# C scaled in two stages, the last attention block in two query parts, and sums that begin in score steps: a planned kernel of state-space model and attention on one core

## The chip, the cores and the metric

The kernel runs on one core of a Trainium2 chip. The metric is the device time of one execution in microseconds (us), as the median of several runs. A core has five engines with a queue of instructions each: PE (TensorE, the matmuls), ACT (ScalarE), DVE (VectorE), POOL (GpSimd) and SP, which here issues most of the transfers.

## What is computed

Two parts that share nothing but the output array, side by side along its last axis.

```python
# A: a diagonal state-space model, L = 2048 steps, 640 states, 640 channels
Lam_bar = exp(dt * Lam);  B_bar = ((Lam_bar - 1) / Lam)[:, None] * Bmat
h = Lam_bar * h + x[t] @ B_bar.T            # complex, step by step
y = 2 * real(hseq @ Cmat.T) + x * Dskip
# B: attention, 32 heads of 20, one key and one value head for all of them
q = (x @ wq) per head;  k = x @ wk;  v = x @ wv
p = softmax(q k^T / sqrt(20));  out = (p v, heads joined) @ wo
```

## The kernel before

**A plan instead of loops.** `planned` (L547) runs a small simulation of the five engines on the host while the program is built. Processes hand in operations (`Op`) with a duration, dependencies and a priority; whenever an engine is free in the model, `pick` takes the ready one with the best priority; the order that comes out is the program, and `Emitter` puts the semaphores in. Durations, priorities and due times are numbers in the code: `STAGES` (L1444) sets some thirty of them anew at certain tile counts, `EARLIER` (L62) says by how many ns before its end an operation that reads PSUM frees its engine (8 for ACT), and a seed moves the due times of the background work by some tiles.

**Attention.** A *tile* is the scores of 128 keys by 512 queries for one head: 4 query blocks x 32 heads x 16 key chunks = 2048 tiles, in 32 blocks of 64 (four heads, 16 chunks). Two slots of three PSUM banks each (`SC0`, `SC1`) take turns. `fill` (L1482) writes two or three tiles of scores into a slot, in the rows of four 32-row matmuls (QT, KT) that run beside each other; ACT turns them into weights in PR by one exp of 1024 or 1536 columns (L1519). Some tiles go to DVE instead: a first pass (`fill_d`, L1717; the rows `BIG<-SC` and `BIG<-MB` of L864) adds and clamps the scores as integers, whose bits are then read as bf16, and three shifted copies follow, by DVE in pairs or singly (`BIG<-BIG`) or by POOL (L1834). Such a tile has four weighted sums with values scaled four ways (VS), a tile of ACT's one (VP). Where DVE's tile sits in the third bank of a slot, that slot's next fill waits for its first pass. `pv_source` (L1851) groups the weighted sums by four: 32-column matmuls beside each other that add up one block in the bank `pvbank` over all of its tiles. DVE copies the block out to `pvsb`, and denominators and head rows go over DRAM to the tiles OP (`normalize`); for the last two blocks `den_task` (L1976) does it on PE: a matmul with E gathers the denominators, DVE takes the reciprocal, a matmul with `ident` spreads it, and DVE multiplies by halves. `o_task` (L2009) multiplies by WO (by WOt, kept in BT, for the last two blocks); in the last query block the parts for output tiles 0, 2 and 4 that don't need the last block are summed early and parked in BA (`EARLY_O`).

**Background.** The state-space part runs as tasks of one PSUM bank each, taken by their due times, in tile numbers: units (x times B, rotation and scan on DVE) and the y sums. C is needed in two scaled forms, G2 C and G C (complex factors per state). `scale_c` (L2265) makes both on DVE, two scalings of four operations (`scaled`, L2226) for each of five chunks: CA gets G2 C, then CT is scaled in place by G, with scratch in W[1]. Only then, from tile 358 on, `cb_task` (L2308) multiplies CT with B: ten products CB, which y needs too. The load of WO is issued behind tile 200.

**Two modes of PE.** Score steps use 32-row tiles, nearly all else 32-column tiles; the plan charges for a change of mode. A task may put pieces of its sums into the free row of a score step (`ride`, `board`: a "ride"), but only after its first product has been made in a step of its own. `keep_source` (L936) adds empty matmuls (VZ) where PE has had little to do.

The lines that touch the prediction's steps most:

```python
            a = self.scaled(xa, x, sc[:, self.G2RE, c:c + 1], sc[:, self.G2IM, c:c + 1], True, (ck, ak), q, "qt", cts + [sc_op] + prev, 3)
            b = self.scaled(x, x, sc[:, self.GRE, c:c + 1], sc[:, self.GIM, c:c + 1], True, (ck, ck), q, "qt", a, 3)
...
            if r.last is None:
                continue
```

Of the kernel before, what the change touches and what calls it, by code (L numbers as in the profile page):

```python
# [46 lines left out]
class Schedule:  # L47
# [14 lines left out]
    EARLIER = {"dve": 40.0, "act": 8.0}  # L62
# [397 lines left out]
NTILE = NQB * NGG * NKC * 4  # L460
ALPHA = float(DH) ** -0.5
# [5 lines left out]
class Build:  # L467
# [45 lines left out]
    def lay_banks(self):  # L513
# [11 lines left out]
        self.rest, self.pvbank = rest, rest[-1]  # L525
        self.misc = rest[:self.MISC]
        self.early = [b for b in self.banks if b not in rest]

    def shared(self):
# [9 lines left out]
        shares.update({f"DR{self.NDS + i}": over for i, over in enumerate(self.dr_over)})  # L539
        shares["WOt"] = [f"BT{i}_{c}" for i in range(2) for c in range(NC)]  # L540
# [4 lines left out]
    SEEDS, REPLAYS = (10005,), 12  # L545
# [256 lines left out]
    def piece(self, r, out, lhsT, rhs, row):  # L802

        tag = object()
        r.end = tag
        at = slice(32 * row, 32 * row + 32)
        return lambda e: e.matmul(out, lhsT=lhsT[at], rhs=rhs[at], start=False, stop=r.end is tag,  # L807
                                  tile_position=(32 * row, 0), skip_group_check=True)

    def board(self, op, used):  # L810
# [5 lines left out]
        for r in self.rides:  # L816
            if r.last is None:
                continue
# [16 lines left out]
            fns = [self.piece(r, *m, x) for m in step[0]]  # L835
# [15 lines left out]
    OPEN = 1  # L851
# [15 lines left out]
    def program(self):  # L867
# [21 lines left out]
        self.pvq = {b: [[], [], [], []] for b in range(NQB * NGG)}  # L889
        self.pv_filled = {b: 0 for b in range(NQB * NGG)}  # L890
# [45 lines left out]
    def keep_source(self):  # L936

        b = self.pv_b
        if not self.started or b >= NQB * NGG or not all((b, j) in self.pv_first for j in range(4)):
            return None  # L940
        if self.pv_filled[b] == 64 and sum(len(q) for q in self.pvq[b]) < self.KEEP_Q:
            return None
# [80 lines left out]
    def loads(self):  # L1023
# [40 lines left out]
        for o, t in zip(self.vec_op + self.xn_op + [self.wk_op, self.wqa_op, self.wv_op, self.wq_op], self.LANDS):  # L1064
# [11 lines left out]
                       gate=lambda: self.tile_n > 200)  # L1076
# [358 lines left out]
    def rules(self):  # L1435

        while self.stages and self.stages[0][0] <= self.tile_n:
# [8 lines left out]
            648.138, 'WAITING': 3, 'REFILL': 905.623, 'SPARE': 148.045, 'LAG': 190.385, 'SOON': 2730.774, 'EARLIER': 4, 'LATER':  # L1446
            7, 'AHEAD': 10, 'CAP': 3, 'ROOM': 4, 'ALONE': 1.397, 'TASK': 0.95, 'PV': 2.034, 'EV': 0.52, 'P1': 0.5, 'COPY': 0.554,
            'COPY1': 0.836, 'P1OWN': 0.42, 'PVEV': 0.209, 'SCARCE': 8, 'BACKLOG': 9, 'GRACE': 55.439, 'SHARE': 0.29, 'MISC_FIRST':
            0}),
        (250, {'ALONE': 2.237, 'PV': 1.984, 'COPY1': 0.897}),  # L1450
        (500, {'STAY': 1.083, 'SPARE': 86.026, 'SOON': 2941.52, 'ALONE': 2.429, 'TASK': 0.989, 'PV': 1.9, 'P1': 0.519, 'PVEV':
            0.2, 'SCARCE': 7, 'BACKLOG': 7, 'SHARE': 0.301}),
        (850, {'STAY': 1.2, 'dve': 185.73, 'MARGIN': 628.898, 'REFILL': 766.143, 'SPARE': 148.045, 'LAG': 240.378, 'SOON':
            2730.774, 'ALONE': 1.449, 'TASK': 0.95, 'PV': 1.889, 'EV': 0.544, 'P1': 0.5, 'SCARCE': 8, 'BACKLOG': 9}),
        (1200, {'STAY': 0.876, 'MARGIN': 648.138, 'REFILL': 905.623, 'LAG': 190.385, 'ALONE': 2.13, 'PV': 1.718, 'EV': 0.506,
            'COPY': 0.534, 'COPY1': 0.9}),
        (1600, {'STAY': 1.2, 'pe': 196.33, 'EARLIER': 5, 'ALONE': 1.525, 'PV': 1.9, 'COPY': 0.554, 'COPY1': 0.897, 'P1OWN': 0.321,
            'GRACE': 41.523}),
# [23 lines left out]
    def fill(self, op, i):  # L1482
# [18 lines left out]
        for x, m in enumerate(tiles):  # L1501
            b, kc, j = self.score(op, m, t[:, 512 * x:512 * x + 512], banks[x])
            ents.append((b, kc, j, p.PR[:, h.index + x, :]))
# [26 lines left out]
        for (b, kc, j, rhs), key in zip(ents, keys):  # L1530
            self.pvq[b][j].append((p.VP[:, kc, 0:32], kc, rhs, key, ex, h, "VP"))
# [73 lines left out]
    def score(self, op, m, out, bank):  # L1605
# [5 lines left out]
        op.fns.append(self.mm(out, p.KT[32 * j:32 * j + 32, 128 * kc:128 * kc + 128],  # L1611
                              p.QT[32 * j:32 * j + 32, b % 12, :], True, True, tile_position=(32 * j, 0)))
        op.reads += [f"KT{kc // 4}", f"QT{b % 12}"] + ([f"QTr{b % 12}"] if b > 1 else [])
        op.writes.append(bank.key)
        return b, kc, j
# [101 lines left out]
    def fill_d(self, op, m, bank=None):  # L1717
# [8 lines left out]
        b, kc, j = self.score(op, m, bank.ap, bank)  # L1726
# [15 lines left out]
    def pv_entry(self, b, kc, j, k, h, op):  # L1742
        self.pvq[b][j].append((self.VS[:, k, kc, 0:32], kc, self.dr(h.index, BF16), f"DR{h.index}", op, h, "VS"))
# [19 lines left out]
    def copy_source(self):  # L1763
# [8 lines left out]
        if sum(len(d[2]) for d in can) < self.BACKLOG and not (can[0][3] == self.pv_b and self.pv_filled[self.pv_b] == 64):  # L1772
            return None
# [9 lines left out]
        if can[0][3] == self.pv_b and self.pv_filled[self.pv_b] == 64:  # L1783
# [8 lines left out]
    LAST = 16  # L1792
    POOL_LAST = 25
# [57 lines left out]
    def pv_source(self):  # L1851
        b = self.pv_b
        if b >= NQB * NGG or not self.started:
# [9 lines left out]
        for j in range(4):  # L1863
            can = [e for e in q[j] if e[4].end is not None and s.seen(e[4], "pe") <= t and self.vp_seen(e[1], t)]
# [4 lines left out]
        complete = self.pv_filled[b] == 64 and not any(self.d_left[b, j] for j in range(4))  # L1869
        left = sum(len(x) for x in q)  # L1870
        tight = self.tight()
        if len(group) < 4 and not tight and not (complete and left < 12 and len(group) == sum(1 for x in q if x)):
            return None
        prio = 0.9 if tight or complete else self.PV
# [6 lines left out]
    def pv(self, op, b, group):  # L1881
        p = self
        bank = self.pvbank
        for j, e in group:
# [4 lines left out]
            last = self.pv_filled[b] == 64 and not self.pvq[b][j] and not self.d_left[b, j]  # L1889
# [726 lines left out]
```

## Time and profile before

| what | us |
|---|---|
| median of three runs | 701.93 (701.88 to 702.15) |
| profiled execution: its time | 701.27 |
| its span, first to last instruction | 699.5 |
| first exp starts | 18.2 |
| last exp ends | 691.2 |

One execution was recorded. In the rows that the prediction shows, a group has its line, engine and operation, the tile written and those read, the shapes and a count, then the busy time in us and the mean duration of one in ns, and last the idle time of the engine just before them with what ended it. Rows in order of time begin with start and length in us, and an idle time in brackets. SC are the slots' banks, MB the two single ones. Matmuls that run beside each other in parts of the array have a row for each, so their durations don't add up to time.

### The profile page before, as it was taken

How to read it: one execution, taken by the hardware profiler on the slowest of the kernel's cores; microseconds unless marked ns; L12 is line 12 of the kernel's file. 1: busy time of each engine (PE TensorE's matmuls, PEld its weight loads, DVE VectorE, ACT ScalarE, POOL GpSimd, SP SyncE). 2: the span in 40 equal slices, each digit the busy share in tenths (PEclk: the TensorE clock that was granted, in tenths of full speed). 3: DMA queues.
4: the chain of work that ended last, by engine and by line, in shares of the span. 5: the costliest groups of instructions: out<-in, count | busy, mean ns of one | idle time of the engine just before them, and what ended most of it. 6: DMA issues, size and time to landing. Idle time of an engine off the chain costs nothing.

```text
span 699.5 us, 27013 instructions
## 1 busy us (share of the span) xinstructions
PE 684.9 (98%) x11350; PEld 248.1 (35%) x11350; DVE 630.2 (90%) x1211; ACT 685.4 (98%) x701; POOL 467.7 (67%) x796
## 2 busy tenths in 40 slices
PE   9999999999999999999999999999999999999997
PEld 5323232334323333534343323334333333343323
DVE  7899899999999988898979997899999999997695
ACT  7999999999999999999999999999999999999996
POOL 4266776443868898464777885767866777768780
PEclk9999999999999999999999999999999999999999
DMA  9649831101111111000030010120000011100101
GB/s 220 174 107 211 184 89 58 28 8 31 28 48 32 28 43 37 22 19 16 17 83 20 15 42 21 36 55 22 12 15 20 12 26 39 32 20 15 27 15 40
DMA packets 77590, 34.46 MB, mean 49 GB/s; under 512 B 58350, under 2 KB 77470, under 8 KB 77470
## 3 DMA queue, kind: packets, MB, share of 16 engines
q1 hardware_dynamic: 76506, 32.44, 19.3%
q8 instruction: 91, 1.49, 0.9%
q10 hardware_dynamic: 964, 0.29, 0.2%
q14 instruction: 29, 0.24, 0.1%
HBM read 11.53 MB, written 9.75 MB: 30 GB/s over the span
## 4 chain that ended last, share of the span: by engine, by line
PE 66%; ACT 33%; DVE 0%; issue 0%; DVEq 0%
ACT PR L1519 33%; PE MB L727 26%; PE MB L797 17%; PE SC L727 14%; PE MB L807 7%; PE SC L1155 1%; PE MB L723 1%; PE SC L723 0%; DVE PR L859 0%; PE MB L1272 0%; DVE mab L1161 0%; DVEq L510 0%; PE SC L1211 0%; DVE pvsb L859 0%; DVE M L863 0%
## 5 line engine op out<-in xcount | busy, mean ns | idle before, releaser
L1519 ACT ACTIVATE PR<-SC 128x1024 bf16<-128x1024 f32 (+1 forms) x677 | 670.5, 1177 | 4.0 <-PE SC L727 2.9
L1834 POOL INT64_ADD BIG<-BIG x761 | 455.4, 614 | 200.8 <-DVE BIG L864 71.8
L864 DVE TENSOR_SCALAR BIG<-SC 128x512 int16<-128x512 f32 x548 | 369.1, 684 | 48.9 <-PE SC L727 42.6
L727 PE MATMUL SC<-QT,KT 32*128 32x512 bf16 x2013 | 264.5, 384 | 7.0 <-ACT PR L1519 6.0
L727 PE MATMUL MB<-BIG,VS 128*32 128x512 bf16 x2332 | 257.4, 383 | 0.4 <-DVE pvsb L1901 0.2
L727 PE MATMUL MB<-PR,VP 128*32 128x512 bf16 x1465 | 213.7, 384 | 0.0
L727 PEld LDWEIGHTS SC<-QT,KT 32*128 32x128 bf16 x2013 | 66.6, 91 | 157.4 <-ACT PR L1519 94.5
L727 PEld LDWEIGHTS MB<-BIG,VS 128*32 128x32 bf16 x2332 | 61.6, 95 | 65.1 <-issue 40.2
L727 PEld LDWEIGHTS MB<-PR,VP 128*32 128x32 bf16 x1465 | 51.4, 94 | 44.6 <-issue 32.5
L797 PE MATMUL MB<-CT,W 128*32 128x320 bf16 (+2 forms) x996 | 52.6, 301 | 0.6 <-issue 0.6
L864 DVE TENSOR_SCALAR BIG<-BIG 128x1024 int16<-128x1024 int16 (+1 forms) x116 | 45.8, 427 | 1.7 <-PE MB L727 1.3
L807 PE MATMUL MB<-xaT,BT 32*128 32x256 bf16 x200 | 38.6, 272 | 0.7 <-ACT PR L1519 0.6
L797 PE MATMUL MB<-CA,W 128*32 128x512 bf16 (+1 forms) x640 | 35.5, 302 | 0.0
L797 PE MATMUL MB<-xaT,BA 128*32 128x256 bf16 x800 | 32.2, 275 | 0.0
L807 PE MATMUL MB<-diagD,xaT 32*128 32x128 bf16 x320 | 31.4, 217 | 0.0
L807 PEld LDWEIGHTS MB<-diagD,xaT 32*128 32x128 bf16 x320 | 17.7, 92 | 28.9 <-ACT PR L1519 19.3
L797 PEld LDWEIGHTS MB<-CT,W 128*32 128x32 bf16 x996 | 22.4, 96 | 15.2 <-issue 7.5
L2086 DVE CAST stg<-MB 128x512 bf16<-128x512 f32 x35 | 23.9, 682 | 2.5 <-PE MB L797 2.5
L797 PE MATMUL MB<-xaT,BT 128*32 128x256 bf16 x600 | 25.1, 274 | 0.0
L859 DVE TENSOR_TENSOR prod<-MB,tab 128x1024 bf16<-128x1024 f32 x20 | 24.3, 1217 | 0.4 <-PE MB L797 0.2
L864 DVE TENSOR_SCALAR BIG<-MB 128x512 int16<-128x512 f32 x35 | 23.8, 679 | 0.0
L2353 DVE TENSOR_TENSOR_SCAN g<-sc,hst,prod 128x256 bf16<-128x256 f32 x30 | 22.9, 774 | 0.1
(174 smaller groups left out, 488.3 us busy)
## 6 DMA issues: line engine op xcount, KB each, us to landing
out_dram<-stg SPq DMA_DIRECT2D x31, 128.0 KB, 1.8
qd<-BIG SPq DMA_DIRECT2D x20, 128.0 KB, 2.4
QT<-qd SPq DMA_DIRECT2D x28, 80.0 KB
OP<-pvsb SPq DMA_DIRECT2D x105, 20.0 KB
rdP<-recs SPq DMA_DIRECT2D x105, 20.0 KB
lbd<-BA SPq DMA_DIRECT2D x5, 320.0 KB, 4.0
CT<-in_B_x_dram SPq DMA_DIRECT2D x2, 640.0 KB, 5.3
BA<-in_A_B_re_dram SPq DMA_DIRECT2D x1, 800.0 KB, 7.0
```

The lines of the kernel that those rows point to most:

```text
L723: r = e.matmul(out[32 * j:32 * j + 32], lhsT=lhsT[:, 32 * j:32 * j + 32], rhs=rhs, start=start, stop=stop, tile_position=(0, 32 * j), skip ...
L727: return lambda e: e.matmul(out, lhsT=lhsT, rhs=rhs, start=start, stop=stop, **kw)
L797: x = e.matmul(out[32 * j:32 * j + 32], lhsT=lhsT[:, 32 * j:32 * j + 32], rhs=rhs, start=start, stop=r.end is tag, tile_position=(0, 32 * ...
L807: return lambda e: e.matmul(out, lhsT=lhsT[at], rhs=rhs[at], start=False, stop=r.end is tag, tile_position=(32 * row, 0), skip_group_check ...
L859: return lambda e: e.tensor_tensor(out, a, b, op)
L864: return lambda e: e.tensor_scalar(out, a, s1, s2, op0=op0, op1=op1)
L1155: prev = self.pe([lambda e, x=x, c=c, n=n, at=at: e.matmul(bank.cols(n * x, n * x + n), lhsT=p.wks[:, 128 * c:128 * c + 128], rhs=p.xbT[:, ...
L1519: ex = self.act(lambda e: e.activation(dst, t[:, 0:512 * n], ACT.Exp, scale=1.0 / UNIT), 0.8333 * 512 * n + 64, table="exp", deps=[op], re ...
L1834: op.fns.append(lambda e: e.int64_add(words(dst), words(src), add))
L2086: ev = self.dve(lambda e: e.tensor_copy(st, bank.ap), 645, deps=[prev], reads=[bank.key], writes=[key], prio=self.EV, gate=(lambda: last.e ...
L2353: o = self.dve(lambda e, ri=ri, init=init: e.tensor_tensor_scan(p.g[:, u, ri, :], rdec, p.prod[:, 1, 0, ri, :], init, ALU.mult, ALU.add), ...
```

## The change

1. **C in two stages.** CA gets G C first, for all five chunks; CB is made from CA. The second stage scales CT in place by G2, at a lower priority, due at tile 400, with scratch in WO, so WO is loaded only after it. CB is due from tile 172 on. The y sums take the two forms from the other array each.
2. **The tail in two query parts.** The last block's tiles are 256 queries of two key chunks, so that one half of the queries is complete after half of the block's tiles; evacuation, denominators and output of the halves are apart. Only output tiles 2 and 4 have an early part; tiles 0 and 1 wait for the left half alone.
3. **Sums may begin in score steps** (`BEGIN`): the first piece of a task may be a ride.
4. **The model takes an exp at full length** (`EARLIER` of ACT 0 instead of 8 ns), other numbers in `STAGES`, and another seed.

```diff
-    EARLIER = {"dve": 40.0, "act": 8.0}
+    EARLIER = {"dve": 40.0, "act": 0.0}
...
-    SEEDS, REPLAYS = (10005,), 12
+    SEEDS, REPLAYS = (169732,), 12
...
-            if r.last is None:
+            if r.last is None and (not self.BEGIN or any(d.end is None or s.seen(d, "pe") > s.t for d in r.bank.last)):
                 continue
...
-            fns = [self.piece(r, *m, x) for m in step[0]]
+            fns = [self.piece(r, *m, x, start=r.last is None and not i) for i, m in enumerate(step[0])]
...
-                       gate=lambda: self.tile_n > 200)
+                       gate=lambda: self.c_more is not None and self.s.done(self.c_more))
...
-        (1200, {'STAY': 0.876, 'MARGIN': 648.138, 'REFILL': 905.623, 'LAG': 190.385, 'ALONE': 2.13, 'PV': 1.718, 'EV': 0.506,
-            'COPY': 0.534, 'COPY1': 0.9}),
+        (1200, {'STAY': 0.876, 'PAUSE': 500.0, 'dve': 233.993, 'MARGIN': 696.79, 'REFILL': 905.623, 'LAG': 230.879, 'SOON':
+            2154.193, 'ALONE': 2.13, 'PV': 1.756, 'EV': 0.506, 'COPY1': 0.9, 'PVEV': 0.2, 'BACKLOG': 8}),
...
+    @staticmethod
+    def parts(b, r):
+
+        if b < LASTB:
+            return [(0, r, 0, 512)]
+        return [(256 * x, 2 * (r % 8) + x, 256 * (r // 8), 256) for x in range(2)]
...
-    LAST = 16
-    POOL_LAST = 25
+    LAST = 12
+    POOL_LAST = 14
...
+            elif b == LASTB:
+                ev = self.dve(lambda e: e.tensor_copy(p.pvsb[:, 1, 0:256], bank.cols(0, 256)), 380, deps=[op], reads=[bank.key],
+                              writes=["pvsb1"], prio=self.PVEV, gate=free)
             else:
-                self.evac_op[b] = [
-                    self.act(lambda e: e.activation(p.pvsb[:, slot, :], bank.ap, ACT.Copy), 600, deps=[op],
-                             reads=[bank.key], writes=[f"pvsb{slot}", f"pvsb{slot}r"], prio=0.1, gate=free)]
+                ev = self.act(lambda e: e.activation(p.pvsb[:, 1, 256:512], bank.cols(256, 512), ACT.Copy), 380, deps=[op],
+                              reads=[self.pvright], writes=["pvsb1r"], prio=0.1)
...
-    EARLY_O = (0, 2, 4)
+    EARLY_O = (2, 4)
...
-            a = self.scaled(xa, x, sc[:, self.G2RE, c:c + 1], sc[:, self.G2IM, c:c + 1], True, (ck, ak), q, "qt", cts + [sc_op] + prev, 3)
-            b = self.scaled(x, x, sc[:, self.GRE, c:c + 1], sc[:, self.GIM, c:c + 1], True, (ck, ck), q, "qt", a, 3)
-            prev = b
-            ops += a + b
+            prev = self.scaled(xa, x, sc[:, self.GRE, c:c + 1], sc[:, self.GIM, c:c + 1], True, (ck, ak), q, "qt",
+                               list(self.ct_op) + [sc_op] + prev, 3)
+            ops += prev
+        more = []
+        for c in range(NC):
+            x, ck = p.CT[:, :, c, :], [f"CT0_{c}", f"CT1_{c}"]
+            prev = self.scaled(x, x, sc[:, self.G2RE, c:c + 1], sc[:, self.G2IM, c:c + 1], True, (ck, ck), p.WO[:, 0:2, :], "qc",
+                               [sc_op] + prev, 3.4)
+            more += prev
+        self.c_more = more
+        self.s.spawn(self.hurry(self.C2_DUE, more))
...
-    CB_FROM, CB_STEP = 358.689, 15.665
+    C_DUE, C2_DUE = 200, 400
+    CB_FROM, CB_STEP = 172.381, 11.308
...
-                    m, mk = (p.CT, f"CT{ri}_{c}") if eo else (p.CA, f"CA{c}")
+                    m, mk = (p.CA, f"CA{c}") if eo else (p.CT, f"CT{ri}_{c}")
```

Three places show how the order moves. **DVE, before, in the last third of the scaling.** A row has line, operation, tile written and tiles read, and its size; `CA<-CT,sc` and `CT<-CT,sc` are products with the factors, W is scratch.

```order
L864 TENSOR_SCALAR W<-CT,sc 128x1280
L859 TENSOR_TENSOR OP<-OP,rdP 128x512
L864 TENSOR_SCALAR BIG<-BIG 128x2x512
L863 TENSOR_SCALAR CA<-CT,sc 128x2x640
L859 TENSOR_TENSOR prod<-prod 128x512
L859 TENSOR_TENSOR CA<-CA,W 128x640
L859 TENSOR_TENSOR CA<-W,CA 128x640
L2353 SCALAR_TENSOR_TENSOR g<-sc,prod 128x256
L864 TENSOR_SCALAR W<-CT,sc 128x1280
L863 TENSOR_SCALAR CT<-CT,sc 128x2x640
```

**DVE, after, the end of the first stage**, the fifth chunk:

```order
L867 TENSOR_SCALAR W<-CT,sc 128x1280
L867 TENSOR_SCALAR BIG<-SC 128x512
L866 TENSOR_SCALAR CA<-CT,sc 128x2x640
L867 TENSOR_SCALAR BIG<-SC 128x512 x2
L1316 CAST BIG<-MB 128x512
L862 TENSOR_TENSOR CA<-CA,W 128x640
L867 TENSOR_SCALAR BIG<-SC 128x512
L862 TENSOR_TENSOR CA<-W,CA 128x640
```

Two scalings stood close together without a first pass (`BIG<-SC`) between them; now four first passes stand inside one scaling, and the scalings of the second stage (`WO<-CT,sc`) follow between later ones. In all, 47 first passes stood between the first and the last scaling operation of 40; now 32 stand inside the first stage and 34 inside the second.

**ACT, before, exps 104 to 146**, and then **after, exps 104 to 149**; 128x1024 is a two-tile exp, 128x1536 a three-tile one:

```order
L1519 ACTIVATE PR<-SC 128x1024 x6
L1519 ACTIVATE PR<-SC 128x1536
L1519 ACTIVATE PR<-SC 128x1024 x5
L1519 ACTIVATE PR<-SC 128x1536 x2
L1519 ACTIVATE PR<-SC 128x1024 x2
L1519 ACTIVATE PR<-SC 128x1536 x10
L1519 ACTIVATE PR<-SC 128x1024 x5
L1519 ACTIVATE PR<-SC 128x1536 x8
L1519 ACTIVATE PR<-SC 128x1024 x4
```

```order
L1527 ACTIVATE PR<-SC 128x1536
L1527 ACTIVATE PR<-SC 128x1024 x7
L1527 ACTIVATE PR<-SC 128x1536
L1527 ACTIVATE PR<-SC 128x1024 x2
L1527 ACTIVATE PR<-SC 128x1536
L1527 ACTIVATE PR<-SC 128x1024 x3
L1527 ACTIVATE PR<-SC 128x1536 x3
L1527 ACTIVATE PR<-SC 128x1024 x14
L1527 ACTIVATE PR<-SC 128x1536 x5
L1527 ACTIVATE PR<-SC 128x1024 x9
```

Of 43 exps 21 had three tiles; of 46 now 11 have.

**PE, before, behind the last weighted sum** (`PR,VP`), and then **after**; `E` gathers denominators, `ident` spreads their reciprocals, `WO,OP` and `BT,pvsb` are the output's sums:

```order
L727 MATMUL MB<-PR,VP 32x512 x3
L723 MATMUL SC<-WO,OP 32x512 x16
L723 MATMUL SC<-BT,pvsb 32x512 x4
L723 MATMUL SC<-E,pvsb 32x4 x16
L723 MATMUL SC<-WO,OP 32x512 x12
L727 MATMUL SC<-ident,rdT 32x128 x16
L723 MATMUL SC<-WO,OP 32x512 x4
L723 MATMUL SC<-BT,pvsb 32x512 x12
L723 MATMUL SC<-BT,pvsb 32x128 x16
L723 MATMUL SC<-BT,pvsb 32x512 x8
```

```order
L1943 MATMUL MB<-PR,VP 32x256 x4
L726 MATMUL SC<-WO,OP 32x512 x16
L726 MATMUL SC<-E,pvsb 32x4 x8
L726 MATMUL SC<-BT,pvsb 32x512 x8
L726 MATMUL SC<-WO,OP 32x512 x4
L726 MATMUL SC<-ident,rdT 32x128 x8
L726 MATMUL SC<-WO,OP 32x512 x12
L726 MATMUL SC<-BT,pvsb 32x128 x16
L726 MATMUL MB<-BT,pvsb 32x512 x4
L726 MATMUL SC<-BT,pvsb 32x512 x8
L726 MATMUL SC<-WO,OP 32x512 x16
L726 MATMUL SC<-BT,pvsb 32x512 x8
```

The denominators' matmuls are half as many, the output sums of tiles 0, 1 and 3 stand whole behind the last weighted sum, and those of tile 3 come last.

More of the change, by code (lines that the diff above doesn't have):

```diff
@@ L460 @@
 NTILE = NQB * NGG * NKC * 4
+LASTB = NQB * NGG - 1
 ALPHA = float(DH) ** -0.5
@@ L1910, in pv, with pv_fn, fn @@
             self.pv_gate = list(self.evac_op[b])
+    def pv_fn(self, b, j, v, kc, rhs, first, last):
+        p, bank = self, self.pvbank
+        parts = self.parts(min(b, LASTB), kc)
+        def fn(e):
+            for i, (lo, c, at, n) in enumerate(parts):
+                r = e.matmul(bank.tensor[32 * j:32 * j + 32, bank.off + at:bank.off + at + n], lhsT=v[:, c, 0:32], rhs=rhs[:, lo:lo + n],
+                             start=first and not i, stop=last and i == len(parts) - 1, tile_position=(0, 32 * j), skip_group_check=True)
+            return r
+        return fn
     LATE_DMA = 2000.0
```

167 lines of the change are left out of this document (95 added, 72 removed).

## The prediction

> **What bounds the kernel now.** First the page's busy shares and its groups, then ScalarE's exps apart by shape, then the stretch from the first exp to the last beside the end behind it.
>
> ```profile
> PE 684.9 (98%) x11350; PEld 248.1 (35%) x11350; DVE 630.2 (90%) x1211; ACT 685.4 (98%) x701; POOL 467.7 (67%) x796
> ...
> L1519 ACT ACTIVATE PR<-SC 128x1024 bf16<-128x1024 f32 (+1 forms) x677 | 670.5, 1177 | 4.0 <-PE SC L727 2.9
> ```
>
> ```profile
> L1519 ACT ACTIVATE PR<-SC 128x1024 bf16<-128x1024 f32 x566 | 532.9, 1106 | 4.0 <-PE SC L727 2.9 <-PE MB L727 0.7
> L1519 ACT ACTIVATE PR<-SC 128x1536 bf16<-128x1536 f32 x111 | 160.2, 1538 | 0.0
> ```
>
> ```profile
> 18.00:691.50 673.50, 664.39 (x11113) 236.34 (x11113) 614.01 (x1151) 670.48 (x677) 459.62 (x769) 1.00 0.19 44
> 691.50:699.50 8.00, 3.94 (x108) 1.81 (x100) 2.89 (x6) 1.79 (x3) 0.00 (x0) 0.92 0.29 84
> ```
>
> The columns of the last fence are length, then busy us of PE, PEld, DVE, ACT, POOL, then granted clock, DMA share, GB/s. Two engines show 98%, but matmul ends are modelled, so PE's figure proves little. ACT's does: 677 exps in one row, with 4.0 us of idle time in all. What one exp occupies isn't its mean duration, since neighbours overlap; it comes from a run of equal ones:
>
> ```profile
> 18.16 22.11 ACT L1519 ACTIVATE PR<-SC 128x1024 bf16<-128x1024 f32 x24 [1.45 <-PE SC L727]
> ```
>
> These 24, all of two tiles, take 22.11 us: **0.92 us for a two-tile exp**. A three-tile one lasts 1538 - 1106 = 0.43 us longer, so **1.35**. Check: 566 x 0.92 + 111 x 1.35 = 520.7 + 149.9 = 670.6, the busy time of the row. The exp row therefore *is* the stretch, and the stretch is 96% of the span.
>
> Does PE have room beside it? One cycle near the end:
>
> ```profile
> 667.30 0.39 PE L727 MATMUL SC<-QT,KT 32*128 32x512 bf16 x3
> 667.62 0.39 PE L727 MATMUL MB<-PR,VP 128*32 128x512 bf16 x1
> ...
> 667.85 0.38 PE L727 MATMUL MB<-BIG,VS 128*32 128x512 bf16 x1
> ...
> 668.17 0.39 PE L727 MATMUL SC<-QT,KT 32*128 32x512 bf16 x3
> ```
>
> Scores start at 667.30, two groups of four sums follow at 667.62 and 667.85, and the next scores start at 668.17: 0.87 us with some 0.1 us of waiting, against 0.92 for the exp. A third group adds about 0.22 and overshoots. So ACT leads, and PE is close behind.
>
> Last, the hole where ACT does what DVE can't:
>
> ```profile
> L864 DVE TENSOR_SCALAR W<-CT,sc x10: 527/539/903, 86.7 to 156.6; 128x1280 bf16<-128x1280 bf16 x10
> ```
>
> ```profile
> L1519 ACT ACTIVATE PR<-SC 128x1536 bf16<-128x1536 f32 x21 | 28.9, 1571 | 0.0
> L1519 ACT ACTIVATE PR<-SC 128x1024 bf16<-128x1024 f32 x14 | 13.7, 1158 | 0.0
> ```
>
> ```profile
> 123.00:163.00 40.00, 37.10 (x645) 14.80 (x645) 38.51 (x82) 39.99 (x35) 15.93 (x26) 1.00 0.11 26
> ```
>
> C is scaled from 86.7 us until about 159. From 123 to 163 DVE is busy 38.51 of 40 us, and 21 of 35 exps have three tiles: DVE has no time for its third of the tiles, so ACT pays 1.35 us for three tiles where 0.92 would do.
>
> **The change, part by part.**
>
> *Exps.* Counted in the order, 566 + 111 become 579 two-tile, 98 three-tile and 1 one-tile exp; 1465 tiles become 1453. At 0.92, 1.35 and 0.92 - 0.43 = 0.49 us: 532.7 + 132.3 + 0.5 = 665.5, against 670.6. **-5.1 us**, on the path, and certain as far as ACT stays without gaps. The rows quoted with the change show where: 11 three-tile exps stand where 21 did. The model's own numbers (the ACT entry of `EARLIER`, the stages' table, the seed) issue nothing: what they do is in these counts. The work of scaling is as large as before; only half of it stands ahead of the CB products, and the other half lies between DVE's first passes.
>
> *DVE.* Its part of the tiles grows by 12:
>
> ```profile
> L864 DVE TENSOR_SCALAR BIG<-SC 128x512 int16<-128x512 f32 x548 | 369.1, 684 | 48.9 <-PE SC L727 42.6 <-PE MB L727 0.6
> ...
> L864 DVE TENSOR_SCALAR BIG<-BIG 128x1024 int16<-128x1024 int16 x111 | 44.8, 434 | 1.7 <-PE MB L727 1.3
> ...
> L864 DVE TENSOR_SCALAR BIG<-BIG 128x512 int16<-128x512 int16 x5 | 1.2, 278 | 0.0
> ```
>
> 12 first passes x 0.67 (369.1/548) = 8.1; 16 more pair copies x 0.40 = 6.5; 4 more single copies x 0.24 = 1.0; less about 0.7 at the end: +15 us, since POOL's copies stay at 761. DVE's 614 become 629 in a stretch of some 668: its idle time falls from 59 to 39 us. Hidden as long as no bank waits for a first pass.
>
> *PE.* In matmuls of 512 columns: scores stay 2048; weighted sums rise by 36 (three more for each of 12 tiles); of the other column-tiled work, 40 move into free rows of score steps (275 to 315, since sums may begin there), where they cost nothing. Net -4, or -1 group. Fillers, which only keep PE active, fall by 88 of 256 columns:
>
> ```profile
> L727 PE MATMUL MB<-KT,VZ 128*32 128x256 bf16 x228 | 10.1, 274 | 0.0
> ```
>
> 22 groups at about 0.11: -2.4 us, of which nothing counts where PE waited anyway. So PE's useful work stays while ACT's falls by 5.1: **PE's lead over the exps shrinks**. I let ACT's idle time rise from 4.0 to 4.5 (+0.5). The bounds: -2, if rides and the early CB products fill the gaps better; +5, the whole gain of ACT, if PE keeps its pace.
>
> *The end.* Behind the last exp stand:
>
> ```profile
> 688.39 2.85 ACT L1519 ACTIVATE PR<-SC 128x1536 bf16<-128x1536 f32 x2
> ...
> 695.99 0.60 ACT L2081 ACTIVATE PR<-SC 128x512 bf16<-128x512 f32 x1 [0.46 <-PE SC L723]
> ```
>
> ```profile
> 690.59 0.60 PE L727 MATMUL MB<-BIG,VS 128*32 128x512 bf16 x8
> ...
> 691.51 1.04 PE L723 MATMUL SC<-WO,OP 128*32 128x512 bf16 x16
> ...
> 693.78 1.75 PE L723 MATMUL SC<-BT,pvsb 128*32 128x512 bf16 x36
> ```
>
> 16 matmuls take 1.04 and 8 take 0.60, so four take 0.22. The end now is 8.3 us (691.24 to 699.5), and PE runs 691.51 to 695.53, 4.0 us, of which 15 groups (60 matmuls, with 16 of 128 columns as four) are 3.3: the rest waits for the normalizing chain. After the change 20 groups stand there (48 of WO, 32 of BT): output tile 0 has no early part any more. 4.4 us plus some 0.25 for the denominators: 4.65, with no waiting, since the left half's work fills the right half's chain. **+0.6**. Bounds: -0.8, if the shorter chain (256 columns in evacuation and product, a one-tile last exp) is what counts, and +1.2, if both add up.
>
> *Moved transfers.* The WO load leaves its place on SP's queue:
>
> ```profile
> L797 PE MATMUL MB<-WO,OP x436: 219/379/391, 227.4 to 584.5; 128*32 128x512 bf16 x77, 128*32 128x128 bf16 x69
> ...
> L707 SPq DMA_DIRECT2D WO<-in_B_wo_dram x1: 425/425/425, 97.4 to 97.4; - x1
> ```
>
> Now it follows the second stage, which ends behind 121 of 595 first passes, a fifth of the way, near 155 us (18 + 673 x 0.2). First use is at 227.4, at almost the same score number (627 against 621). Some 70 us cover it: nothing. The sums of y now wait for the second stage too, but the first of them stand behind 690 of 2048 scores, a third of the way, so nothing queues there either.
>
> *Sum.* -5.1 + 0.5 + 0.6 = -4.0. Profiled execution: 701.27 - 4.0 = 697.3. The median of the runs, 701.93, is 0.66 above that execution, so I forecast **697.9**.
>
> **Rivals.**
>
> *PE takes over as the bound.* For it: the 0.87 us cycle, useful work that stays. Against it: 4.0 us of idle ACT time at almost the same PE load. Then only the fillers' 2.4 and the one group come off, with the end's +0.6: 701.93 - 2.6 + 0.6 = **699.9**.
>
> *DVE takes over, slower.* Where a fill's third bank holds DVE's tile, the bank comes free by DVE's first pass; a late pass holds the fill and so ACT. For it, in the last stages ACT loses most:
>
> ```profile
> 508.00:578.00 70.00, 69.56 (x1113) 23.94 (x1101) 68.56 (x126) 69.64 (x73) 49.66 (x84) 1.00 0.07 19
> 578.00:648.00 70.00, 68.98 (x1185) 24.64 (x1185) 63.97 (x117) 68.56 (x71) 52.31 (x89) 1.00 0.11 28
> ```
>
> Against it: at 68.56 us of DVE in 70 ACT lost 0.36 us, and the 1.44 fall where DVE had six to spare. If every 70 us lost 1.44, 9.6 such stretches lose 13.8 instead of 4.5: 697.9 + 9.3 = **707.2**. It is slower than before from an ACT idle time of about 10 us on.
>
> *TensorE loses its clock.* Fillers fall by 22 groups. In the table the clock is 1.00 through the stretch and 0.92 only behind the last exp, where PE works 3.94 of 8 us. At half clock the streaming part of a cycle, 3 x 0.21, doubles: 0.87 becomes 1.5, and 7 us of exps take 4.5 more: 697.9 + 4.5 = **702.4** for one such stretch, and two are clearly slower. Against it, the stretch that lost fillers, 123 to 163 us, now has CB products instead. The Trainium skill speaks for this rival: its page "TensorE: Matmul & The Clock Gate", section "What's actually happening", says that the gate falls to half after an idle window of about 3.4 us. The trace shows no such drop ahead of 691.5, so what counts as idle inside a dense stretch no run here shows.
>
> *The end gains instead*, with -0.8 there and 2 us less idle: 701.93 - 5.1 - 2 - 0.8 = **694.0**.
>
> **How the numbers follow.** Forecast 60%, its own range 695.5 to 700; PE bound 17% (699 to 701.5); DVE late 12% (703.3 to 707); clock 4%; the better end 7%. The range leaves out the upper part of DVE's case, most of two clock drops and a sliver at the low end: 694.3 to 702.5. A measurement here can tell 0.2%, 1.4 us, so "same" is 700.5 to 703.3. Faster: 60 + 7 + 10 of PE's 17 = 77%. Same: the other 7 and, of the clock's 4, 3: 10%. Slower: 12 + 1 = 13%.
>
> **What would show it.** Right: exps of 579, 98 and 1 in a busy row near 665.5 with 3 to 6 us of idle time; few three-tile exps between 123 and 163 us; the last exp ending near 686.6; 8 to 9.5 us behind it with PE busy throughout; PE's clock 1.00. Wrong: idle ahead of the exps over 10 us, released by PE behind long runs of sums (PE's rival) or with PE's scores waiting for DVE's first passes (DVE's); a stretch under clock 1.00; an end under 8 us. The forecast falls if ACT's idle time takes back the 5.1.

## The result and the profile after

The changed kernel takes **697.84 us** (median of 5 runs, 696.98 to 698.27), the kernel before 701.93 (701.61 to 702.21, 5 runs): a ratio of 0.9943, 95% interval 0.9932 to 0.9954. The profiled execution took 697.64 us, its span is 695.8; the one of before took 701.27, with a span of 699.5, so the two profiles are 3.7 apart where the medians are 4.1 apart.

The page after, busy time of the engines and the group of all exps (last the idle time ahead of them, with what ended it):

```profile
PE 684.4 (98%) x11492; PEld 251.8 (36%) x11492; DVE 637.2 (92%) x1243; ACT 681.9 (98%) x703; POOL 469.0 (67%) x796
...
L1527 ACT ACTIVATE PR<-SC 128x1024 bf16<-128x1024 f32 (+1 forms) x678 | 666.6, 1130 | 4.1 <-PE SC L1623 2.9
```

The same group after, by shape:

```profile
L1527 ACT ACTIVATE PR<-SC 128x1024 bf16<-128x1024 f32 x579 | 544.6, 1067 | 3.6 <-PE SC L1623 2.5 <-PE MB L1623 0.3 <-PE MB L1943 0.2
L1527 ACT ACTIVATE PR<-SC 128x1536 bf16<-128x1536 f32 x98 | 141.5, 1506 | 0.5 <-PE SC L1623 0.4
L1527 ACT ACTIVATE PR<-SC 128x512 bf16<-128x512 f32 x1 | 0.7, 698 | 0.0
```

The counts are the forecast's. The busy time is 666.6 where it said 665.5, the idle time 4.1 where it said 4.5. Now the stretch of the exps, the end behind it, and the former hole (columns as before: length, busy us of PE, PEld, DVE, ACT, POOL, granted clock, DMA share, GB/s):

```profile
18.60:687.90 669.30, 662.41 (x11248) 238.84 (x11244) 621.86 (x1185) 666.60 (x678) 460.91 (x769) 1.00 0.19 44
687.90:695.80 7.90, 4.98 (x118) 2.74 (x110) 1.92 (x4) 2.17 (x4) 0.00 (x0) 1.00 0.30 85
...
123.00:163.00 40.00, 39.61 (x640) 14.12 (x636) 36.08 (x73) 40.00 (x40) 22.65 (x39) 1.00 0.19 46
```

The stretch from the first exp's start (18.69) to the last one's end (687.90) is 669.2 us, it was 673.1: **-3.9**. The end is 7.9, it was 8.3: **-0.4**. The first exp starts 0.5 later, with the same order of instructions on ACT, DVE and POOL ahead of it; in the profiles of all runs here it starts between 18.0 and 18.9, so that is scatter. From 123 to 163 us DVE is busy 36.1 us instead of 38.5, PE 39.6 instead of 37.1, and 10 of the 40 exps have three tiles, where 21 of 35 had.

### The profile page after: what moved, and what is told of

Read it like the earlier page. It is cut to its first block, busy times and chain, and to the rows that moved or that the text cites. A ratio compares the mean times of both kernels' runs of the same rounds, so it can differ in the third digit from the quotient of the medians.

```text
span 695.8 us, 27396 instructions
## 1 busy us (share of the span) xinstructions
PE 684.4 (98%) x11492; PEld 251.8 (36%) x11492; DVE 637.2 (92%) x1243; ACT 681.9 (98%) x703; POOL 469.0 (67%) x796
## 4 chain that ended last, share of the span: by engine, by line
PE 57%; ACT 41%; DVE 1%; issue 0%
ACT PR L1527 41%; PE MB L1943 21%; PE MB L800 14%; PE SC L1623 10%; PE MB L810 8%; PE MB L730 1%; DVE BIG L867 1%; PE SC L1159 1%; PE SC L726 1%; PE MB L726 0%; PE SC L730 0%; DVE pvsb L1922 0%; PE MB L1276 0%; DVE mab L1165 0%; DVE prod L862 0%
## 5 line engine op out<-in xcount | busy, mean ns | idle before, releaser
L1527 ACT ACTIVATE PR<-SC 128x1024 bf16<-128x1024 f32 (+1 forms) x678 | 666.6, 1130 | 4.1 <-PE SC L1623 2.9
L867 DVE TENSOR_SCALAR BIG<-SC 128x512 int16<-128x512 f32 x560 | 376.1, 684 | 37.7 <-PE SC L1623 32.0
L1943 PE MATMUL MB<-BIG,VS 128*32 128x512 bf16 (+1 forms) x2468 | 269.5, 376 | 0.9 <-DVE pvsb L1922 0.9
L1623 PE MATMUL SC<-QT,KT 32*128 32x512 bf16 (+1 forms) x2073 | 265.6, 378 | 4.4 <-ACT PR L1527 1.8
L1943 PE MATMUL MB<-PR,VP 128*32 128x512 bf16 (+1 forms) x1495 | 222.2, 378 | 0.1
L1943 PEld LDWEIGHTS MB<-BIG,VS 128*32 128x32 bf16 x2468 | 68.3, 95 | 65.1 <-issue 40.4
L867 DVE TENSOR_SCALAR BIG<-BIG 128x1024 int16<-128x1024 int16 (+1 forms) x136 | 52.3, 418 | 0.9 <-PE MB L1943 0.4
L800 PE MATMUL MB<-CA,W 128*32 128x320 bf16 (+2 forms) x992 | 51.5, 300 | 0.8 <-DVE BIG L2363 0.4
L810 PE MATMUL MB<-xaT,BT 32*128 32x256 bf16 x192 | 37.1, 273 | 0.0
L800 PE MATMUL MB<-CT,W 128*32 128x512 bf16 (+1 forms) x640 | 36.1, 302 | 0.0
L800 PEld LDWEIGHTS MB<-CA,W 128*32 128x32 bf16 x992 | 22.9, 96 | 14.7 <-issue 6.2
```

The source lines that it names most:

```text
L800: x = e.matmul(out[32 * j:32 * j + 32], lhsT=lhsT[:, 32 * j:32 * j + 32], rhs=rhs, start=start, stop=r.end is tag, tile_position=(0, 32 * ...
L867: return lambda e: e.tensor_scalar(out, a, s1, s2, op0=op0, op1=op1)
L1527: ex = self.act(lambda e: e.activation(dst, t[:, 0:512 * n], ACT.Exp, scale=1.0 / UNIT), 0.8333 * 512 * n + 64, table="exp", deps=[op], re ...
L1623: r = e.matmul(out[:, bank.off + lo:bank.off + lo + n], lhsT=p.KT[32 * j:32 * j + 32, 128 * c:128 * c + 128], rhs=p.QT[32 * j:32 * j + 32, ...
L1943: r = e.matmul(bank.tensor[32 * j:32 * j + 32, bank.off + at:bank.off + at + n], lhsT=v[:, c, 0:32], rhs=rhs[:, lo:lo + n], start=first an ...
```

## The experiments

Order and mixture of the exps come out of the plan, and each plan hangs on its seed. So a variant with another plan takes the best of the same 150 seeds, the one whose plan ends first in the model; before and after get such controls too. The differences below are against the kernel before, timed on the same chip. *Theory A* in the expectations is the prediction's: ACT's exps set the time. The other numbers of the change (`STAGES`) were not tried apart, and neither were sums begun in score steps, or the model's exp at full length, put into the kernel before alone.

| kernel | two-, three-tile exps | median us | before | ratio, 95% interval |
|---|---|---|---|---|
| before, other seed | 572, 107 | 701.39 | 701.36 | 1.0003 (0.9994 to 1.0012) |
| after, other seed | 584, 95 | 698.35 | 701.36 | 0.9958 (0.9944 to 0.9972) |
| before, the same other seed, tail in two parts | 572, 107 | 700.86 | 701.36 | 0.9993 (0.9984 to 1.0003) |
| after without the tail in two parts, another seed | 572, 103 | 700.66 | 701.36 | 0.9983 (0.9973 to 0.9992) |
| after without the tail in two parts, its own seed | 579, 99 | 698.96 | 701.40 | 0.9965 (0.9952 to 0.9978) |
| after, C in one stage | 572, 106 | 702.99 | 701.40 | 1.0018 (1.0008 to 1.0027) |
| before, C in two stages | 581, 100 | 701.80 | 701.40 | 1.0007 (0.9997 to 1.0017) |
| after, no sums begun in score steps | 586, 97 | 703.56 | 701.40 | 1.0030 (1.0020 to 1.0040) |
| before, exps at 496 of 512 columns | as before | 697.66 | 701.06 | 0.9951 (0.9936 to 0.9966) |
| after, exps at 496 of 512 columns | as after | 695.32 | 701.06 | 0.9920 (0.9905 to 0.9935) |
| after, short fillers | as after | 697.15 | 701.06 | 0.9951 (0.9934 to 0.9967) |
| after, exps 8 ns shorter in the model | 553, 122 | 705.19 | 701.06 | 1.0059 (1.0044 to 1.0074) |

### Other seeds

```diff
-    SEEDS, REPLAYS = (10005,), 12
+    SEEDS, REPLAYS = (105,), 12
```

> The kernel before with another seed, the one of 150 whose plan ends first in the model. Its plan has 572 two-tile and 107 three-tile exps: 572 x 0.92 + 107 x 1.35 = 670.7 us of exps, against 670.6 of before. Theory A, ACT's exps bound the time: as before, 702.0 (700.6 to 703.4), with 3 to 6 us of idle time in the row of the exps. Theory B, the time hangs on how well PE and the other engines fill the plan, and the seed of before was a lucky one: slower by 2 us or more, the surplus in idle time ahead of the exps.

For after the seed is 44:

> The kernel after with another seed, the best of the same 150. Its plan has 584 two-tile and 95 three-tile exps: 665.5 us, the same as after's plan. Theory A: as after, 697.8 (696.4 to 699.2), so that the gain belongs to the change and not to after's seed. Theory B: 699.5 or more, the exps' idle time at 6 us or above; the gain against the other-seed kernel of before would then be well under 4.

Both as theory A had it: 701.39, and 698.35 or 3.0 below before. With the one other seed that was tried 3 of the 4 us are there. That after's own seed is worth the fourth is not shown: the two were timed on different chips, and their intervals overlap (0.9932 to 0.9954 and 0.9944 to 0.9972).

### The tail

Before with the tail's hunks alone, and after with them taken out (with two seeds); the core of the edit:

```diff
-    EARLY_O = (0, 2, 4)
+    EARLY_O = (2, 4)
...
+    def parts(b, r):
```

> The kernel before, with the seed of the other-seed kernel, and with the tail in two query parts alone. Plan and exps up to the last block are the same as in that kernel (572 and 107, 670.7 us), so the difference between the two is the end. From the profile after (end of the last exp to the end of the span 7.9 us against 8.26): -0.4 against the other-seed kernel, PE busy without a pause behind the last exp for 4.9 us. Rival, the prediction's own figure: +0.6. A third case, the left half's evacuation and sums that move ahead of the last exps cost ACT there: the end shorter, but the last exp later by as much.

> The kernel after without the tail's two parts (one evacuation, three early parts, as before), best seed of 150. Its plan has 572 two-tile and 103 three-tile exps: 526.2 + 139.1 = 665.3 us. Theory A: exps as after, the end as before, 698.1 (697 to 699.5): nearly the whole gain is there without the tail. Rival, the tail is a part of the gain above 1 us: 699.5 or more, the surplus behind the last exp.

> The kernel after without the tail's two parts, with after's own seed: the same plan as after up to the last block (579 two-tile and 99 three-tile exps; 666.3 us of exps against 665.5, since the last block's tiles are cut otherwise). So the difference from after is the tail alone. Theory A: +0.8 of exps and the +0.5 by which the kernel of before was slower than with the tail in two parts: 1.3 us above after, that is 2.7 below before. Rival, the tail is worth 2 us or more in this plan (the other seed without it came out at only 0.7 below before): 0.7 below before, the surplus behind the last exp, where PE waits for the one evacuation.

In the plan of before: 700.86 against 701.39, **-0.5**, the -0.4 expected, from ten runs each (their means differ by 0.57, with an uncertainty of about 0.4); the prediction's +0.6 had the wrong sign. First the last two evacuations of the output's sums by ACT in the kernel of before with the other seed; then, in the kernel after, the evacuation of the right half's weighted sums, PE's last matmuls, and the last evacuation:

```profile
695.45 0.60 ACT L2081 ACTIVATE PR<-SC 128x512 bf16<-128x512 f32 x1 [2.60 <-PE SC L723]
696.50 0.60 ACT L2081 ACTIVATE PR<-SC 128x512 bf16<-128x512 f32 x1 [0.46 <-PE SC L723]
```

```profile
688.38 0.38 ACT L1928 ACTIVATE pvsb<-MB 128x256 bf16<-128x256 f32 x1 [0.48 <-PE MB L1943]
...
692.27 0.61 PE L726 MATMUL SC<-BT,pvsb 128*32 128x512 bf16 x8
692.93 0.60 ACT L2123 ACTIVATE PR<-SC 128x512 bf16<-128x512 f32 x1 [0.70 <-PE SC L726]
```

PE's work behind the exps is longer, 687.96 to 692.88, without a pause, as worked out. But the last evacuation starts 0.05 us behind the last matmul (692.88 to 692.93), where in the kernel before it lay 0.46 behind (695.53 to 695.99), and from its start to the end of the span are 2.87 us (692.93 to 695.8), where there were 3.51. The kernel before with the tail alone shows the same 0.05 and 2.87. In after's plan the tail is worth some 1.7 (698.96 is 2.4 below before, after 4.1 on its own chip; the bare medians of the two chips differ by 1.1). Besides the end, the exps' stretch is 1.7 longer without it (670.9), in an execution that took 0.8 more than that kernel's median; a three-tile exp in place of a one-tile one explains 0.8. The run with the other seed missed by more: 665.3 us of exps and yet 700.7, where A said 698.1. That was the first sign that the exps' sum does not make the time.

### C in two stages

```diff
-    C_DUE, C2_DUE = 200, 400
-    CB_FROM, CB_STEP = 172.381, 11.308
+    C_DUE = 200
+    CB_FROM, CB_STEP = 358.689, 15.665
```

> The kernel after without the two stages of C (both forms of C ahead of the CB products again, and CB due from tile 358), best seed of 150. Its plan has 572 two-tile, 106 three-tile exps and 1 one-tile exp: 526.2 + 143.1 + 0.5 = 669.8 us. Theory A, the early CB products let DVE take its third of the tiles and that is where the exps go: 0.8 of exps and 0.5 of the end, 1.3 us below before, with some twenty three-tile exps from 123 to 163 us again. Rival, C in two stages is not what brings the gain: 3 us or more below before.

> The kernel before with C in two stages alone, best seed of 150. Its plan has 581 two-tile and 100 three-tile exps: 534.5 + 135.0 = 669.5 us. Theory A, the time goes with the sum of the exps: 1.1 us below before. Rival, C in two stages carries the gain by itself: 3 us or more below before. Third case, the plan's other numbers do not fit it, idle time ahead of the exps rises: no gain, or slower.

Without the two stages all of the gain is gone and more: 1.6 above before and so 5.6 above after (4.0 below before), though the sum of its exps is 0.8 under that of before. In before, two stages alone bring nothing (+0.4): the time of the third case, but not its reason, since the exps' idle time is 3.2 us there and did not rise. The cycles of PE, below, tell where it goes. The former hole in the run without two stages:

```profile
L1526 ACT ACTIVATE PR<-SC 128x1536 bf16<-128x1536 f32 x17 | 23.6, 1536 | 0.0
L1526 ACT ACTIVATE PR<-SC 128x1024 bf16<-128x1024 f32 x20 | 19.5, 1148 | 0.2 <-PE SC L1622 0.2
```

Of 37 exps between 123 and 163 us 17 have three tiles again.

### Sums that begin in score steps, and the model's exp

```diff
-            if r.last is None and (not self.BEGIN or any(d.end is None or s.seen(d, "pe") > s.t for d in r.bank.last)):
+            if r.last is None:
```

> The kernel after, but sums may no longer begin in score steps, best seed of 150. Its plan has 586 two-tile and 97 three-tile exps: 539.1 + 131.0 = 670.1 us. Theory A: 0.5 of exps and 0.5 of the end, 1.0 us below before. Rival, beginning in score steps only moves matmuls that PE had time for: 3 us or more below before.

```diff
-    EARLIER = {"dve": 40.0, "act": 0.0}
+    EARLIER = {"dve": 40.0, "act": 8.0}
```

> The kernel after with the model's old length of an exp (8 ns shorter), best seed of 150. Its plan has 553 two-tile, 122 three-tile exps and 1 one-tile exp: 508.8 + 164.7 + 0.5 = 674.0 us, 8.5 above after's. Theory A, the time goes with the sum of the exps wherever it comes from: 8.5 above after, 706 or 4.5 above before. Rival, what the three-tile exps cost is won back in fewer late starts, since PE gets more time per exp: 702 to 703, about the kernel of before.

The first came out at 703.56, 2.2 *above* before instead of 1.0 below; the second at 705.19, 4.1 above, near A's 4.5. So C's two stages, the sums begun in score steps and the model's longer exp each cost the whole gain when they are taken out of after, and the tail 1.7 of it with after's seed and 3.3 with the other. Put into before alone, the tail brings 0.5 and C nothing; the other two were not put in alone. After's other numbers were made for all of them together: these runs can't share the 4 us out among the edits.

### Shorter exps

```diff
-        ex = self.act(lambda e: e.activation(dst, t[:, 0:512 * n], ACT.Exp, scale=1.0 / UNIT),
...
+            return e.activation(p.PR[:].rearrange("p i n -> p (i n)")[:, 512 * h.index:512 * h.index + 496 * n], t[:, 0:496 * n], ACT.Exp, scale=1.0 / UNIT)
```

By this edit the columns left out are the last 32 of a two-tile exp and the last 48 of a three-tile one, not 16 of each tile; the length is the same.

> The kernel before, its plan unchanged, but every exp behind the first 40 covers 496 of the 512 columns of each tile; the other 16 columns of those weights are left as they were, so a thirty-second of the exps' work is left out. Two-tile exps that follow each other without a pause start 0.904 us apart and three-tile ones 1.330, so a column takes 0.83 ns and a tile 13.3 ns less; for the some 1380 tiles behind the first 40 exps that is 18.4 us. Theory A, ACT alone sets the pace: -18, near 683. Theory B, PE stands close behind (its cycle of 0.87 us, where the shortened exp takes 0.89): a part of it turns into idle time ahead of the exps; with a third to two thirds taken back, -6 to -12, 689 to 695.

> The kernel after with the same shortening of the exps behind the first 40 to 496 columns per tile (a thirty-second of their work is left out): 1370 tiles x 13.3 ns = 18.2 us. Theory A: -18 against after, so about -22 against before. Theory B, PE close behind: -5 to -11 against after, and less of it passes than in the kernel of before, because after has as much to do on PE in a stretch that is 4 us shorter; the two shortened kernels would then stand closer to each other than the 4 us of before and after.

Here theory A falls. 18 us were taken from the exps, and 3.4 (before) and 1.7 us (695.32 against 0.9943 x 701.06 = 697.06) came off: less even than theory B had. The exps of before in that run, by shape:

```profile
L1527 ACT ACTIVATE PR<-SC 128x992 bf16<-128x992 f32 x528 | 487.9, 1011 | 7.2 <-PE SC L727 3.0 <-PE MB L727 1.6
L1527 ACT ACTIVATE PR<-SC 128x1488 bf16<-128x1488 f32 x109 | 149.2, 1438 | 0.7 <-PE SC L727 0.3 <-PE MB L727 0.2
```

Their idle time rose by a few us only, so how can they take nearly as long? Seven exps and the starts of the score steps beside them near the end, first before, then with the shorter exps (start, length):

```profile
663.24 6.61 ACT L1519 ACTIVATE PR<-SC 128x1024 bf16<-128x1024 f32 x7
663.60 0.39 PE L727 MATMUL SC<-QT,KT 32*128 32x512 bf16 x3
664.47 0.39 PE L727 MATMUL SC<-QT,KT 32*128 32x512 bf16 x3
665.56 0.39 PE L727 MATMUL SC<-QT,KT 32*128 32x512 bf16 x3
666.43 0.39 PE L727 MATMUL SC<-QT,KT 32*128 32x512 bf16 x3
```

```profile
659.99 6.48 ACT L1527 ACTIVATE PR<-SC 128x992 bf16<-128x992 f32 x7
660.40 0.39 PE L727 MATMUL SC<-QT,KT 32*128 32x512 bf16 x3
661.27 0.39 PE L727 MATMUL SC<-QT,KT 32*128 32x512 bf16 x3
662.36 0.39 PE L727 MATMUL SC<-QT,KT 32*128 32x512 bf16 x3
663.23 0.39 PE L727 MATMUL SC<-QT,KT 32*128 32x512 bf16 x3
```

PE's steps stand at 0.87, 1.09 and 0.87 us in both: the exps do not move them. 0.87 is a step with two groups of sums behind the scores, 1.09 one with three. In the trace of before 331 cycles have two groups (median 0.869), 107 three (1.085) and 60 four (1.302); with the shorter exps the medians are 0.869, 1.085 and 1.301. So **a cycle of PE**, from one score step to the next, **takes 0.434 us and 0.217 for each group** of four sums beside each other, and some 555 of before's 667 cycles stand within 0.025 us of that.

The page of before had a row that spoke for PE and that the prediction did not use: the chain of work that ended last, followed back from the end of the program, as shares of the span. Before, after, and with the shorter exps in each:

```profile
PE 66%; ACT 33%; DVE 0%; issue 0%; DVEq 0%
```

```profile
PE 57%; ACT 41%; DVE 1%; issue 0%
```

```profile
PE 80%; ACT 16%; DVE 3%; issue 0%; POOL 0%; DVEq 0%
```

```profile
PE 87%; ACT 7%; DVE 5%; issue 1%; POOL 0%
```

The two shortened kernels have the plans of before and after, so the same exps can be set side by side, start against start. From 100 to 200 us 2.9 us were taken from the exps in each; in before 1.2 of them came off the time in that stretch, in after 0.1. (The kernel after and its run with short fillers, of equal plans too, differ there by 0.1, and by 0.3 at most in another 100 us.) So, by these traces, ACT held the program up in part in the former hole, and after the change it does so no longer.

### Where PE's time goes

With this rule each trace can be taken apart: from the first score step to the last, *useful* is 0.434 a cycle and 0.217 a group without the fillers (score steps of more than four tiles, 6 to 13 in a trace, are given 0.054 for each further tile, a quarter of 0.217); the rest is *slack*, waiting and fillers together. It is one execution each, and how the longest steps are divided moves a figure by up to 0.8.

| kernel | first to last cycle, us | useful | slack | of it to 100 us | 100 to 200 | behind 200 |
|---|---|---|---|---|---|---|
| before | 671.0 | 637.5 | 33.5 | 7.5 | 14.8 | 11.2 |
| after | 667.9 | 638.6 | 29.3 | 9.1 | 8.1 | 12.1 |
| before, C in two stages | 669.8 | 637.9 | 31.9 | 7.5 | 10.9 | 13.5 |
| after, C in one stage | 674.2 | 637.4 | 36.8 | 9.1 | 14.8 | 12.9 |
| after, none begun in score steps | 671.8 | 641.1 | 30.7 | 8.6 | 3.6 | 18.5 |
| after, exps 8 ns shorter in the model | 674.7 | 634.8 | 39.9 | 9.3 | 15.3 | 15.3 |
| before, exps at 496 of 512 columns | 667.7 | 637.6 | 30.0 | 7.2 | 13.5 | 9.4 |
| after, exps at 496 of 512 columns | 666.0 | 638.7 | 27.3 | 8.6 | 7.8 | 10.8 |

After's gain sits in one place: from 100 to 200 us PE's slack falls by 6.7; 2.5 of it are given back as slack elsewhere and 1.1 as useful work. That leaves 3.1; the other 0.8 of the exps' 3.9 lie behind the last cycle's start, where the last exp now has one tile. With C in one stage the 14.8 are back. With C in two stages alone they fall to 10.9, and 2.3 come back behind 200 us. Without sums begun in score steps PE has 2.5 us more of useful work, and 6.4 more of slack behind 200 us. Where the plan gives the exps more three-tile steps (exps 8 ns shorter in the model) PE has less to do and more slack; that it waits for the exps there is argued, not shown. Shortened by 18 us, the exps take only 3.5 and 2.0 off the slack. What makes up the 27 to 30 us that stay, beside the fillers, is open. The rows of the busy times from 100 to 200 us say the same, before, after and with C in one stage (first PE):

```profile
100.00:200.00 100.00, 95.45 (x1532) 34.25 (x1522) 95.55 (x188) 99.99 (x97) 57.86 (x97) 1.00 0.14 37
```

```profile
100.00:200.00 100.00, 97.81 (x1612) 35.91 (x1608) 93.25 (x185) 100.00 (x97) 58.54 (x96) 1.00 0.18 45
```

```profile
100.00:200.00 100.00, 95.97 (x1589) 36.24 (x1581) 91.87 (x184) 98.90 (x94) 55.81 (x91) 1.00 0.15 40
```

ACT shows 99 to 100 in all three and tells nothing. A matching run that takes work from PE alone, at full exps, was not tried.

### Fillers

```diff
-         fns = [self.mm(bank.tensor[32 * j:32 * j + 32, bank.off:bank.off + 256], p.VZ[:], p.KT[:, 0:256], False,
+         fns = [self.mm(bank.tensor[32 * j:32 * j + 32, bank.off:bank.off + 8], p.VZ[:], p.KT[:, 0:8], False,
```

> The kernel after, its plan unchanged, with the 144 empty filling matmuls at 8 columns instead of 256; no result is changed by that. Theory A: PE waited at those places anyway, nothing changes (within 0.7 of after), and the granted clock stays 1.00. Rival, PE binds there too: 35 groups at about 0.11 us, up to -3.8. Rival, the fillers hold the clock: stretches with a granted clock under 1.00, and slower by 4.5 for each stretch of 7 us, as the prediction worked it out.

697.15, where after would be at 697.1 on this chip: nothing, as A had it. The clock in the two stretches with most fillers and in the one behind them:

```profile
18.00:100.00 82.00, 79.92 (x1091) 25.16 (x1095) 77.87 (x182) 81.55 (x83) 46.09 (x78) 1.00 0.65 149
100.00:200.00 100.00, 97.08 (x1612) 35.95 (x1609) 93.34 (x186) 100.00 (x97) 58.67 (x96) 1.00 0.18 46
200.00:300.00 100.00, 99.97 (x1830) 38.28 (x1826) 89.88 (x164) 99.12 (x102) 71.78 (x119) 1.00 0.11 28
```

It is 1.00 there and in the four stretches that follow, up to 687 us. The fillers stand where PE waits anyway.

## Why the prediction was right, and where it was not

**The time was right, the step under it was not.** The prediction said that the exps' row "*is* the stretch" and that "ACT leads, and PE is close behind", from a cycle of "0.87 us with some 0.1 us of waiting". That 0.1 is no waiting: the cycle stays at 0.87 with exps of 0.88, so 0.87 is PE's own time for it. PE goes through most cycles at its own pace, with two groups a little faster than an exp and with three or four slower, and ACT comes late behind the long ones. The check that was to support it, 0.92 x 566 + 1.35 x 111 = the busy time, proved nothing: 0.92 is 22.11 us over 24 exps, some of which already wait (their starts are 0.911 apart on the mean), and it holds the full length of the last one. Exps that are fed on time start 0.904 apart, three-tile ones 1.330, which makes 659.3 for before, 11 under its busy row. A recorded exp begins some 0.2 us before its predecessor ends (it lasts 1.106 on the mean), so a late start eats into this overlap and doesn't show as idle time. The Trainium skill would have led the same way: its page "Perfetto Trace Analysis", section "Identifying the Most-Contended Engine", takes occupancy for ScalarE, and for TensorE the share of peak FLOPs, which no profile here gives, and the weight loads' share; by the two that the profile of before shows (ACT 98%, PEld 35%) it names ACT. Here the runs decide against it.

**Exps, -5.1.** The counts were right. The stretch fell by 3.9. At shortened exps, where ACT has 18 us to spare, after is still 2.3 ahead (695.32 against 697.66), of which the end is about 0.5. So some 1.8 of the stretch's gain is there without the exps' pace, and some 2 at most hang on it.

**The hole** was named rightly, 123 to 163 us, and so was what closes it: half of the scaling no longer stands ahead of the CB products. It was read as time that ACT lost to three-tile exps. ACT was indeed full there: from 123 to 163 us 30 of 34 exps start as early as they can behind the one before, and with shorter exps about half of what they give up comes off there. By the cycles PE had 14.8 us of slack between 100 and 200 us and now has 8.1. Both are one thing seen from two engines: where DVE is kept from its tiles, PE has fewer sums to do and waits for longer exps (this link is argued from the order, not tested apart). That is why the sum of the exps gave the right size here, and the wrong one for the runs without C's two stages and without sums begun in score steps (off by 2.9 and 3.2).

**PE's useful work stays** was right: 1599.0 groups before, 1598.2 after, by count; the forecast was -1. The fillers' -2.4 is part of the slack, as it said.

**PE takes over** (699.9) was the better picture of the machine with the wrong price: beside one group of sums it let only the fillers come off, since it took the waiting for gone.

**The end, +0.6,** was -0.4: the mis-sized term is what lies behind PE's work. PE's 4.65 became 4.9, but 0.2 went ahead of it, 0.4 between it and the last evacuation, and 0.6 behind that one's start. By the prediction's own list an end under 8 us was a sign of being wrong, and it came: 7.9. The last exp ends at 687.9, not near 686.6.

**DVE, +15,** hidden: right. Its instructions, added up, last 15.6 us longer; the busy time rose by only 7.9 (614.0 to 621.9), since more of them overlap. PE's matmuls waited for first passes for 1.0 us in all, for exps 1.8:

```profile
PE SC L1623 <- ACT PR L1527: 1.8, 7, 0.4
...
PE SC L1623 <- DVE BIG L867: 1.0, 3, 0.5
```

**Moved transfers** cost nothing, as it said, but with less room than it said: the second stage of C ends at 194 us, not near 155, the load of WO is issued at 194.2 and lands 4.9 us later, and its first use is at 232.2.

**TensorE's clock** held at 1.00, even with the fillers cut to 8 columns; the longest pause of PE between two matmuls of the exps' stretch was 0.62 us in that run. Whether the rule of the Trainium skill's page "TensorE: Matmul & The Clock Gate" ("What's actually happening", a window of about 3.4 us) holds, a pause as short as that can't show.

So the errors partly cancelled: -4.6 forecast and -3.9 measured for the stretch, +0.6 and -0.4 for the end. That the forecast met the median within 0.1 us is luck. What sets the balance of PE and ACT cycle by cycle is not fully settled. -18 us of exps and the rule for PE's cycles show PE ahead in most of them; yet 340 of before's 566 two-tile exps start 0.904 us behind the one before, that is, without a wait. The plan with 674.0 us of exps came out near what their sum says, but the chain in its page does not show ACT ahead (PE 71%, ACT 27%).

## What to carry to other kernels

When two engines both show 98%, take work from one of them and look at the time; a busy row whose instructions overlap can hide much of its waiting, and a price that is a mean over the run agrees with the run by construction. Find the engine whose steps keep their length when the other's shrink: its work and its slack, stage by stage, say where a change can bring something. In a plan whose numbers are tuned as a set, a part taken out singly can cost more than it brings singly, as the tail and C's two stages do here, so don't price an edit by its removal alone.

## What the runs showed of the hardware

- An exp's start follows its predecessor's by 0.904 us at 1024 columns, 0.877 at 992 and 1.330 at 1536 when its scores are there: 0.83 ns a column and 0.05 us besides. The Trainium skill's page "Perfetto Trace Analysis", section "Optimizing Scalar/DVE Operations", states about 51 ns for ScalarE on PSUM, and the rows agree.
- A score step of up to four tiles with the change to the sums and back costs PE 0.434 us, four 512-column sums beside each other 0.217, to within a few ns over hundreds of cycles. 0.217 of the 0.434 go beyond the 512 columns, for the two changes between 32-row and 32-column tiles: at each change the starts lie 0.322 us apart, where two groups in the same tiles lie 0.217 to 0.226 apart. That such a change drains TensorE is stated by the Trainium skill's page "TensorEngine Tiling (Array Packing)", section "Key Properties", without a price.
- An empty matmul of 8 columns is still recorded with 166 to 180 ns, half of them with 169 or less; one of 256 with 270 to 283.
